# Inverse roots by Ln and Exp on ScalarE, and the first pairs' value products in four pieces

## The chip, the cores and the metric

The kernel runs on one core of a Trainium2 chip. Its time is device microseconds of one execution. Before the change it is 1099.2 us, the median of three runs (1098.22 to 1101.14); lower is better.

## The reference

```python
def _attn_ref(q, k, v, g_q, g_k):          # q, k, v: 8 x 12 x 448 x 64, float32
    def rmsnorm(x, g):
        rms = np.sqrt(np.mean(x * x, axis=-1, keepdims=True) + 1e-06)
        return x / rms * g
    q_n, k_n = (rmsnorm(q, g_q), rmsnorm(k, g_k))
    scores = 1.0 / np.sqrt(64) * np.matmul(q_n, k_n.transpose(0, 1, 3, 2))
    scores = scores - np.max(scores, axis=-1, keepdims=True)
    attn = np.exp(scores)
    attn = attn / (np.sum(attn, axis=-1, keepdims=True) + 1e-09)
    return np.matmul(attn, v)
def _moe_ref(x, w1, w2, w3, w_out):        # x: 3584 x 768 from the heads, weights 768 x 768, float64
    h = np.maximum(np.maximum(x @ w1, x @ w2), x @ w3)
    return h @ w_out
```

The weights come as 64-bit floats; the kernel turns their bits into 32-bit floats itself.

## The kernel before, in words

Two heads of one batch make a **pair** `g`; there are 48, six to a batch. The 448 queries of a pair are worked in four chunks `c` of 112. Each pair is written out as twelve **beats** (`beat(g, i)`, i from 0 to 11), three to a chunk, and `k = 4 * g + c` counts the chunks. The order of every engine's instructions is the order in which the beats issue them; an engine works its queue strictly in this order. `later(n, work)` issues work at the end of the beat that comes n beats on.

For each chunk, TensorE makes the scores of both heads (L545 or L553) into one of two buffers, VectorE takes the row maxima (L562), ScalarE scales them (L570) and makes two exponentials with their sums (L579). The scores of a chunk are issued one chunk ahead.

The first six pairs (`PLAIN = 6`, the **plain** pairs) work in float32: rows of keys and queries are transposed by TensorE (`turn_whole`, L463) and copied by ScalarE (`keep_whole`, L475 and L477), the exponentials are transposed by TensorE (L602) and copied (L611), and the value products (`add_values`, L692) are made in one block of eight matmuls in beat 4 of the next pair. Their result in `av` is multiplied by the inverse sums, which take this way: `guard_sums` (L619, ScalarE, beat 1), `inverse_sums` (L623, VectorE, beat 2), `spread_sums` (L631, TensorE, beat 5), `keep_sums` (L641, ScalarE, beat 6, the tile `by`), `scale_plain` (L711, VectorE, beat 8). `finish` (L717 ScalarE, L718 VectorE one beat later) splits the result into two float16 halves `xt`. From pair 6 on the work is in float16 halves: `upper_weights` (L648 and L652 on VectorE, L655 on ScalarE), `lower_weights` (L665 on VectorE), transposes by DMA; the values are scaled by GpSimd (L517) in beat 9 and cast by ScalarE (L525) in beat 11.

The norms of pair g + 2 are made while pair g runs: `squares` (L365, GpSimd) in beats 0 and 3, `sum_squares` (L372, VectorE) in beats 2 and 5, `inv_rms` in beats 5 and 7. The last is two GpSimd instructions each for keys and for queries, a scaling (L383) and a power with the exponent -0.5 (L387). `scale_k` (L419, L423) and `scale_q` (L394) follow in beats 8 and 9 on GpSimd. Pairs 0 and 1 are made ahead of the first beat, pair 0 with its squares on ScalarE and its scaling on VectorE.

Beside that runs the decoding of the weights, a block every four beats up to pair 5 and every eight then: SP loads `raw` (two buffers), ScalarE rescales it (L188), VectorE decodes it in three steps (L196, L200, L205), and for the input weights ScalarE (L268, L269) and GpSimd (L272) split it into halves. The feed-forward matmuls (L732, L796) are put into the beats by a fixed table of thirds once a batch's six pairs are done, from pair 6 on.

## Time and profile before

| | |
|---|---|
| median of three runs | 1099.2 us |
| profiled execution, its own time | 1099.43 us |
| span of the profiled execution | 1097.6 us |
| TensorE busy | 1011.4 us (92%) |
| VectorE busy | 755.7 us (69%) |
| ScalarE busy | 771.8 us (70%) |
| GpSimd busy | 704.2 us (64%) |
| powers on GpSimd (L387, 96 of them) | 154.2 us |

The shares are averages over parts with different limits, so they are read by stretches of the span. In rows of groups stand the count of instructions, their busy time and the mean of one in ns. In rows of a timeline stand start and length in us, and in brackets the idle time ahead with what ended it. Rows of waits give who waited for whom, the total in us, the number of times and the longest.

### The profile page before, as it was taken

The numbers are of one execution on the slowest core, as the hardware profiler recorded it, in microseconds if no ns is written. First come the engines' busy times: TensorE is split into PE (matmuls) and PEld (weight loads), VectorE is DVE, ScalarE is ACT, GpSimd is POOL, SyncE is SP. The second block draws the span as 40 slices with busy tenths as digits, with TensorE's granted clock in tenths as the row PEclk, the third lists the DMA queues.
The fourth block names the chain that finished last, engine by engine and source line by source line (L and its number), as shares of the span: only waits on it lengthen the run. The fifth ranks groups of instructions, "written<-read, shape, count | busy, mean of one in ns | idle before, by whom it ended". The sixth has DMA issues, their size and how long they took to land. (4 is left out here: it accounts for less than half of the span.)

```text
span 1097.6 us, 18387 instructions
## 1 busy us (share of the span) xinstructions
PE 1011.4 (92%) x6168; PEld 499.4 (45%) x6168; DVE 755.7 (69%) x1390; ACT 771.8 (70%) x1767; POOL 704.2 (64%) x805
## 2 busy tenths in 40 slices
PE   4678769888899999999999999999999999999998
PEld 2333334334444454444544454444444554445554
DVE  4799988888767676777677767777676766761110
ACT  4598888767878687787877787777777787863101
POOL 5477988866767777677777776777777677610000
PEclk9697869999999999999999999999999999999999
DMA  5554566855887779778887798787877797553002
GB/s 152 164 168 149 131 183 135 192 116 121 164 156 143 145 153 179 152 148 144 168 156 147 138 168 172 148 145 155 174 145 140 140 178 142 108 100 73 1 1 57
DMA packets 426493, 152.28 MB, mean 139 GB/s; under 512 B 372896, under 2 KB 422048, under 8 KB 426400
## 3 DMA queue, kind: packets, MB, share of 16 engines
q1 hardware_dynamic: 425888, 150.95, 67.7%
q8 instruction: 48, 0.79, 0.3%
q14 instruction: 45, 0.37, 0.1%
q10 hardware_dynamic: 512, 0.18, 0.1%
HBM read 51.97 MB, written 11.01 MB: 57 GB/s over the span
## 5 line engine op out<-in xcount | busy, mean ns | idle before, releaser
L732 PE MATMUL acc<-xt,w_sb 128*128 128x448 f16 x2592 | 516.8, 355 | 0.0
L732 PEld LDWEIGHTS <-w_sb 128*128 128x128 f16 x2592 | 244.1, 98 | 259.3 <-issue 47.9
L579 ACT ACTIVATE sc<-sc,nm,down 112x448 f32<-112x448 f32 x336 | 234.2, 697 | 11.2
L562 DVE TENSOR_REDUCE sc<-sc 112x2 f32<-112x896 f32 x192 | 209.6, 1092 | 46.0 <-PE sc L553 44.7
L655 ACT ACTIVATE pp<-sc,rs 112x448 f16<-112x448 f32 x336 | 194.8, 632 | 46.6 <-ACT sc L579 40.9
L665 DVE SCALAR_TENSOR_TENSOR pp<-sc,rs,pp 112x448 f16<-112x448 f32 x336 | 212.9, 675 | 3.4 <-ACT pp L655 2.9
L387 POOL TENSOR_TENSOR ri<-ri,half_neg 128x7 f32<-128x7 f32 x96 | 154.2, 1606 | 8.0
L553 PE MATMUL sc<-kt,qt 64*112 64x448 f16 x1008 | 131.9, 367 | 28.8 <-DVE pp L665 25.0
L570 ACT ACTIVATE nm<-sc,down 112x2 f32<-112x2 f32 x192 | 50.7, 264 | 147.5 <-DVE sc L562 146.1
L796 PE MATMUL acc<-wo_sb,ht 128*128 128x384 f16 x864 | 151.0, 329 | 1.5 <-DVE ht L756 0.8
L761 POOL COPY hx<-ht 128x128 f16<-128x128 f16 x48 | 15.5, 323 | 197.1 <-DVE ht L756 191.1
L796 PEld LDWEIGHTS <-ht 128*128 128x128 f16 x864 | 81.6, 99 | 67.2 <-issue 13.5
L703 PE MATMUL av<-pt,vp 128*64 128x448 f16 x1008 | 108.3, 356 | 0.0
L553 PEld LDWEIGHTS <-qt 64*112 64x112 f16 x1008 | 54.8, 126 | 98.3 <-issue 57.8
L648 DVE TENSOR_SCALAR rs<-sc 112x2 f32<-112x2 f32 x168 | 26.6, 158 | 94.6 <-ACT sc L579 94.6
L440 POOL TENSOR_TENSOR kp<-kn,kp 128x512 f16<-128x512 f32 x42 | 50.0, 1191 | 58.9 <-ACT kp L434 58.9
L703 PEld LDWEIGHTS <-vp 128*64 128x64 f16 x1008 | 49.6, 108 | 55.7 <-issue 30.0
L718 DVE SCALAR_TENSOR_TENSOR xt<-av,xt 128x448 f16<-128x448 f32 x42 | 26.2, 625 | 70.8 <-ACT xt L717 70.8
L372 DVE TENSOR_REDUCE ss<-sq 128x7 f32<-128x448 f32 x96 | 60.9, 635 | 10.6 <-ACT sq L363 6.6
L531 POOL TENSOR_TENSOR vp<-vr,vp 128x448 f16<-128x448 f32 x42 | 43.8, 1044 | 30.3 <-ACT vp L525 30.2
L440 POOL TENSOR_TENSOR qp<-qn,qp 112x512 f16<-112x512 f32 x42 | 49.2, 1173 | 19.8 <-ACT qp L434 19.8
L517 POOL TENSOR_SCALAR vr<-vr,v_up 128x448 f32<-128x448 f32 x42 | 61.1, 1456 | 0.0
(112 smaller groups left out, 1200.4 us busy)
## 6 DMA issues: line engine op xcount, KB each, us to landing
raw<-in_moe_w_dram SPq DMA_DIRECT2D x18, 768.0 KB, 4.5
qr<-in_q_dram SPq DMA_DIRECT2D x48, 224.0 KB, 3.1
vr<-in_v_dram SPq DMA_DIRECT2D x96, 96.0 KB, 2.6
kr<-in_k_dram SPq DMA_DIRECT2D x95, 96.0 KB, 3.1
raw<-in_moe_w_out_dram SPq DMA_DIRECT2D x6, 768.0 KB, 5.0
pt<-pp SPq DMA_TRANSPOSE x168, 4.0
out_dram<-osb SPq DMA_DIRECT2D x8, 336.0 KB, 3.2
out_dram<-osb SPq DMA_DIRECT2D x8, 288.0 KB, 3.6
```

The source lines that it names most:

```text
L372: nc.vector.tensor_reduce(sums[g % 2][:sq.shape[0], KQ[what]], sq, axis=AX, op=ALU.add)
L387: nc.gpsimd.tensor_tensor(out=ri, in0=ri, in1=half_neg[:, at], op=ALU.pow)
L440: nc.gpsimd.tensor_tensor(out=parts[:, 1], in0=n, in1=parts[:, 0], op=ALU.subtract)
L517: nc.gpsimd.tensor_scalar(out=vr, in0=vr, scalar1=v_up[:, g // NP:g // NP + 1], scalar2=None, op0=ALU.mult,)
L553: nc.tensor.matmul(sc[:QP, h, :S], qt[rows, qp, c], kt[rows, kp, KEYS[h]], start=n == 0, stop=n == len(TERMS) - 1,)
L562: nc.vector.tensor_reduce(sc[:QP, 0, S + 8:S + 10], sc[:QP, :, :S], axis=AX, op=ALU.max, negate=True)
L579: nc.scalar.activation(to, sc[:QP, h, :S], AF.Exp, bias=nm[:, h:h + 1], scale=down[:QP], accum_out=total,)
L655: nc.scalar.activation(pp[:, 0, h], sc[:QP, h, :S], AF.Copy, scale=rs[:, h:h + 1])
L665: nc.vector.scalar_tensor_tensor(out=pp[:, 1, h], in0=sc[:QP, h, :S], scalar=rs[:, h:h + 1], in1=pp[:, 0, h], op0=ALU.mult, op1=ALU.subtract,)
L703: nc.tensor.matmul(av[half, :S], vp[rows, group, vpart], pt[rows, 7 * wp + group], start=u == 0 and n == 0, stop=u == 3 and n == len(TERMS ...
L732: nc.tensor.matmul(acc[:, :S], wt[:, wp, c], xs[c][:, xp], start=(c == 0 and n == 0), stop=(c == NCT - 1 and n == 2),)
L796: nc.tensor.matmul(acc[:, :HW], lhs, wo_sb[:, f, wp, half * HW:(half + 1) * HW], start=(f == 0 and n == 0), stop=(f == NFT - 1 and n == 2),)
```

## The change

The change does five things.

- **Powers.** `inv_rms` goes. `mean_squares` (beat 4) scales and shifts all 15 sums of a pair in one instruction, `power` (beat 6) takes Ln and then Exp with a scale of -0.5 on ScalarE, `newton` (beat 8) corrects the result by one Newton step: four small instructions on GpSimd, three on VectorE for pairs 0 and 1. The squares move to beats 0 and 1 and their sums to beats 2 and 3. The table of functions that holds Ln and Exp is chosen at the start.
- **Scale of the plain scores.** The constant part of the scale goes into the gain that the transposed queries are multiplied with, so that plain exponentials take scale 1.0 and their row maxima go straight into `nm`; L570 and the scale tile `down` serve only pairs from 6 on. `prep_gain` moves to beat 4 of pair 0.
- **Value products.** For pairs 0 to 4 the eight matmuls are issued two at a time in beats 4, 7, 8 and 10; `scale_plain` goes to beat 11, and `finish` to the first beat after that.
- **Inverse sums.** The guard goes to beat 10 and the inverse to beat 11 of the pair itself; the spreading matmuls to beat 2 and the copy to beat 4 of the next pair.
- **Start.** Pair 1's powers and scaling are issued in beats 0 and 1; pair 1's transposes come in beats 4 and 7 of pair 0 instead of 1 and 4.

```diff
+    nc.scalar.preload_act_table_set("natural_log_exp_and_others")
     nc.scalar.activation(warm, warm, AF.Exp)
...
-    def inv_rms(g, what):
...
-        nc.gpsimd.tensor_scalar(
-            out=ri, in0=sums[g % 2][:, at], scalar1=1.0 / D / QK_UP ** 2,
-            scalar2=RMS_EPS / QK_UP ** 2, op0=ALU.mult, op1=ALU.add,
-        )
-        nc.gpsimd.tensor_tensor(out=ri, in0=ri, in1=half_neg[:, at], op=ALU.pow)
+    def mean_squares(g):
+        s = st[g]
+        s["ms"] = sb.tile([P, 15], F32, name="ms", bufs=2)
+        (nc.gpsimd if g > 1 else nc.vector).tensor_scalar(
+            out=s["ms"], in0=sums[g % 2], scalar1=1.0 / D / QK_UP ** 2,
+            scalar2=RMS_EPS / QK_UP ** 2, op0=ALU.mult, op1=ALU.add,
+        )
+    def power(g):
+        s = st[g]
+        ri = sb.tile([P, 15], F32, name="ri", bufs=2)
+        nc.scalar.activation(ri, s["ms"], AF.Ln)
+        nc.scalar.activation(ri, ri, AF.Exp, scale=-0.5)
...
+    def newton(g):
...
+        if g > 1:
+            nc.gpsimd.tensor_tensor(out=t, in0=ms, in1=ri, op=ALU.mult)
+            nc.gpsimd.tensor_tensor(out=t, in0=t, in1=ri, op=ALU.mult)
+            nc.gpsimd.tensor_scalar(
+                out=t, in0=t, scalar1=-0.5, scalar2=1.5, op0=ALU.mult, op1=ALU.add
+            )
+            nc.gpsimd.tensor_tensor(out=ri, in0=ri, in1=t, op=ALU.mult)
+            return
...
     def row_max(g, c):
+        if g < PLAIN:
+            to = s["nm", c] = sb.tile([QP, 2], F32, name="nm", bufs=3)
+        nc.vector.tensor_reduce(to, sc[:QP, :, :S], axis=AX, op=ALU.max, negate=True)
     def softmax(g, c):
...
+            nm, by = s.pop(("nm", c)), 1.0
+        else:
+            nm, by = sb.tile([QP, 2], F32, name="nm", bufs=3), down[:QP]
+            nc.scalar.activation(nm, sc[:QP, 0, S + 8:S + 10], AF.Copy, scale=by)
...
+    power(0)
+    newton(0)
     scale_k(0)
...
+    nc.scalar.activation(
+        gain_c, column[:, 0:1], AF.Copy, scale=1.0 / QK_UP ** 2 / float(D) ** 0.5
+    )
...
+    later(0, lambda: power(1))
+    later(1, lambda: newton(1))
+    later(1, lambda: scale_k(1))
+    later(1, lambda: scale_q(1))
+    later(4, prep_gain)
...
+        if g < PLAIN:
+            if i == 10:
+                guard_sums(g)
+            if i == 11:
+                inverse_sums(g)
         if 0 <= w < PLAIN:
             if i == 2:
-                inverse_sums(w)
-            if i == 5:
                 spread_sums(w)
-            if i == 6:
+            if i == 4:
                 keep_sums(w)
-            if i == (8 if w < PLAIN else 9):
+            if i == (8 if w == PLAIN - 1 else 11):
                 scale_plain(w)
+        if 0 <= w < PLAIN - 1 and i in (4, 7, 8, 10):
+            add_values(w, [(4, 7, 8, 10).index(i)])
+        elif w >= PLAIN - 1 and i == (4 if w < PLAIN else 7):
             add_values(w)
...
+        if 0 <= w < PLAIN - 1 and i == 11:
+            later(1, lambda: finish(w, x_of[w // NP]))
...
+            if i in (0, 1):
+                squares(n, "kq"[i])
+            if i in (2, 3):
+                sum_squares(n, "kq"[i - 2])
+            if i == 4:
+                mean_squares(n)
+            if i == 6:
+                power(n)
             if i == 8:
+                newton(n)
                 scale_k(n)
```

The change moves lines of the file: L562 becomes L590, L570 L602, L579 L607, L623 L651, L665 L693, L711 L740, L718 L747, L196 L195, L200 L199, L205 L204, L372 L371. Three places show what the queues become. The rows are in the order in which an engine works them; `x2` is two alike.

VectorE at the start, from pair 1's sums of squares (`ss_87` before, `ss_86` now) to pair 2's, before:

```order
L372 TENSOR_REDUCE ss_87<-sq 128x7
L372 TENSOR_REDUCE ss_87<-sq 112x8
L562 TENSOR_REDUCE sc<-sc 112x2 x2
L372 TENSOR_REDUCE ss_86<-sq 128x7
L170 TENSOR_REDUCE v_rows<-vr 128x1
```

and now:

```order
L371 TENSOR_REDUCE ss_86<-sq 128x7
L371 TENSOR_REDUCE ss_86<-sq 112x8
L378 TENSOR_SCALAR ms<-ss_86 128x15
L590 TENSOR_REDUCE nm<-sc 112x2
L404 SCALAR_TENSOR_TENSOR newton<-ms,ri 128x15
L407 TENSOR_TENSOR newton<-newton,ri 128x15
L408 SCALAR_TENSOR_TENSOR ri<-newton,ri 128x15
L590 TENSOR_REDUCE nm<-sc 112x2
L371 TENSOR_REDUCE ss_85<-sq 128x7
```

Newton's three steps for pair 1 stand between the first two row maxima.

VectorE in a plain pair, where pair 1's products are finished. Before, in pair 2 from beat 8 on (`sc<-sc` is the row maximum):

```order
L562 TENSOR_REDUCE sc<-sc 112x2
L711 TENSOR_TENSOR av<-av,by 128x448
L200 SCALAR_TENSOR_TENSOR w_sb<-raw,w_sb 128x768
L170 TENSOR_REDUCE v_rows<-vr 128x1
L205 SCALAR_TENSOR_TENSOR w_sb<-raw,w_sb 128x768
L718 SCALAR_TENSOR_TENSOR xt<-av,v_up,xt 128x448
```

and now, from beat 11 of pair 2 on (`nm<-sc` is the row maximum):

```order
L590 TENSOR_REDUCE nm<-sc 112x2
L651 RECIPROCAL sum<-sum 112x8
L740 TENSOR_TENSOR av<-av,by 128x448
L195 TENSOR_SCALAR w_sb<-raw 128x768
L258 TENSOR_SCALAR w_most<-most 128x1
L261 RECIPROCAL w_up<-w_most 128x1
L262 TENSOR_SCALAR w_up<-w_up 128x1
L199 SCALAR_TENSOR_TENSOR w_sb<-raw,w_sb 128x768
L747 SCALAR_TENSOR_TENSOR xt<-av,v_up,xt 128x448
L204 SCALAR_TENSOR_TENSOR w_sb<-raw,w_sb 128x768
```

The second half of `xt` moved one beat on and behind other decoding steps, and the reciprocal of the pair's sums now stands right behind a row maximum.

VectorE in a pair from 6 on, around the sums of squares of the queries (`ss_87`, now `ss_86`), before:

```order
L562 TENSOR_REDUCE sc<-sc 112x2
L665 SCALAR_TENSOR_TENSOR pp<-sc,rs,pp 112x448 x2
L648 TENSOR_SCALAR rs<-sc 112x2
L652 RECIPROCAL rs<-rs 112x2
L372 TENSOR_REDUCE ss_87<-sq 112x8
L746 TENSOR_TENSOR acc<-acc,m 128x448
```

and now:

```order
L590 TENSOR_REDUCE sc<-sc 112x2
L693 SCALAR_TENSOR_TENSOR pp<-sc,rs,pp 112x448 x2
L371 TENSOR_REDUCE ss_86<-sq 112x8
L676 TENSOR_SCALAR rs<-sc 112x2
L680 RECIPROCAL rs<-rs 112x2
L775 TENSOR_TENSOR acc<-acc,m 128x448
```

The sum moved from behind the two steps of the weights' sums to ahead of them. SP's loads and DMA transposes keep their order, and there is one table load in the changed program as in the one before.

More of the change, by code (lines that the diff above doesn't have):

```diff
@@ L869, in prep_gain @@
     def prep_gain():
-        nc.vector.tensor_tensor(out=gain, in0=gains[:, 0], in1=gains[:, 1], op=ALU.mult)
         row_largest(g_top[:, 0:1], gain)
@@ L899, in qknorm_attention_maxout_ffn_kernel @@
         )
[L900 to L902 removed]
+    turn_whole(0, "q")
+    nc.scalar.activation(
+        gain_c, column[:, 0:1], AF.Copy, scale=1.0 / QK_UP ** 2 / float(D) ** 0.5
+    )
     for what in "kq":
```

72 lines of the change are left out of this document (29 added, 43 removed).

## The prediction

> **What bounds the kernel now.** I read the page first, then the busy times by stretches, one stretch per pair (cut where the copy of `by`, L641, starts), then the waits of VectorE, then the timelines.
>
> ```profile
> span 1097.6 us, 18387 instructions
> PE 1011.4 (92%) x6168; PEld 499.4 (45%) x6168; DVE 755.7 (69%) x1390; ACT 771.8 (70%) x1767; POOL 704.2 (64%) x805
> ```
>
> ```profile
> 40.40:54.07 13.67, 12.22 (x71) 6.72 (x71) 12.20 (x17) 10.90 (x28) 4.49 (x5) 0.77 0.55 168
> 54.07:71.33 17.26, 13.16 (x86) 6.51 (x86) 16.81 (x24) 16.25 (x40) 11.86 (x12) 1.00 0.55 167
> 71.33:93.30 21.97, 17.66 (x91) 9.01 (x91) 20.60 (x26) 19.35 (x45) 18.73 (x15) 0.77 0.45 142
> 93.30:114.04 20.74, 16.42 (x88) 8.34 (x88) 20.19 (x25) 19.34 (x44) 17.66 (x15) 0.84 0.46 145
> 114.04:136.40 22.36, 15.88 (x80) 7.57 (x80) 20.92 (x25) 19.43 (x45) 20.12 (x18) 0.77 0.61 158
> 136.40:161.72 25.32, 14.60 (x76) 8.35 (x76) 22.20 (x35) 20.13 (x45) 24.13 (x21) 0.68 0.63 164
> ...
> 500.00:700.00 200.00, 197.70 (x1259) 96.93 (x1256) 141.66 (x280) 152.44 (x358) 141.96 (x171) 1.00 0.84 157
> ```
>
> After the stretch come its length and the busy time of PE, PEld, DVE, ACT, POOL. From 500 to 700 us PE works 197.7 of 200: there the matmuls are the bound, and nothing that VectorE, ScalarE or GpSimd gain is worth anything. PE's other idle time lies ahead of that. From 40.40 to 161.72 us the six rows give DVE 112.9 of 121.3 busy: in the plain pairs VectorE is the bound, and only its idle 8.4 us can be won by letting the others run better. Whatever is won there moves the whole PE-bound rest forward, since its order on PE stays as it is.
>
> ```profile
> DVE xt L718 <- ACT xt L717: 4.0, 3, 1.5
> DVE w_sb L196 <- ACT raw L188: 2.0, 1, 2.0
> ...
> DVE av L711 <- ACT by L641: 0.7, 2, 0.3
> ```
>
> These are VectorE's waits in the same 121 us (total, times, longest). The first and the last belong to lines that the change moves.
>
> **The start: nothing.** Pair 0's powers leave GpSimd. The timeline (start, length, engine, line, what ended the idle time):
>
> ```profile
> 0.72 1.28 ACT L133 ACT_TABLE_LOAD   x1 [0.72 <-PEq L1046]
> ...
> 5.80 0.69 DVE L372 TENSOR_REDUCE ss<-sq 112x8 f32<-112x512 f32 x1 [0.46 <-ACT sq L363]
> 9.01 0.35 DVE L419 TENSOR_TENSOR kn<-kr,ri 128x192 f32<-128x192 f32 x1
> 14.66 1.10 DVE L562 TENSOR_REDUCE sc<-sc 112x2 f32<-112x896 f32 x1 [0.23 <-PE sc L545]
> 17.56 0.51 POOL L419 TENSOR_TENSOR kn<-kr,ri 128x192 f32<-128x192 f32 x1
> 18.85 0.29 POOL L423 TENSOR_TENSOR kn<-kr,ri 64x64 f32<-64x64 f32 x1
> 19.17 0.81 SPq L342 DMA_DIRECT2D kr<-in_k_dram  x2
> 35.31 3.42 SPq L223 DMA_DIRECT2D raw<-in_moe_w_dram  x2
> 40.41 0.88 ACT L188 ACTIVATE raw<-raw 128x768 f32<-128x768 f32 x1 [3.60 <-DMA raw<-in_moe_w_dram]
> ```
>
> The last sums are done at 6.49. Mean squares, Ln, Exp and three VectorE steps, six small dependent instructions of some 0.2 us each (priced below), end near 7.9, where `kn` now starts at 9.01: 1.1 us sooner. But pair 1's powers now stand on ScalarE behind the first two exponentials. The first row maximum moves by 0.9 (the column of gains now stands among the transposes) from 14.66 to 13.8 and ends at 14.9; two exponentials (1.4), Ln and Exp (0.5), Newton's three steps (0.6) end at 17.4, where GpSimd's `kn` starts at 17.56 today. The load of `kr` at 19.17 starts as soon as that `kn` has ended (18.85 + 0.29), and behind it SP issues loads without a gap up to the raw weights at 35.31, for which ScalarE stands still until 40.41. So the gain of 1.1 us is given back at 17.5, and at 40.4 I expect 0, with bounds of -1.0 and +0.8. The next row maximum is queued behind Newton's steps on VectorE, and behind that exp(0,1), which has 2 us in hand since its key rows no longer stand ahead of it.
>
> **The plain pairs: -3.8 us.**
>
> The groups of the page (count, busy, mean ns of one) and, for the plain exponentials, those from 20 to 180 us:
>
> ```profile
> L570 ACT ACTIVATE nm<-sc,down 112x2 f32<-112x2 f32 x192 | 50.7, 264 | 147.5 <-DVE sc L562 146.1
> ...
> L579 ACT ACTIVATE e<-sc,nm,down 112x448 f32<-112x448 f32 x46 | 32.9, 719 | 0.8
> ```
>
> Two rows of the view of L717 (shortest, median, longest ns), and two of GpSimd's groups:
>
> ```profile
> L717 ACT ACTIVATE xt<-av x42: 535/543/545, 192.8 to 1005.7; 128x448 f16<-128x448 f32 x42
> L717 ACT ACTIVATE xt<-av,v_up x6: 627/630/634, 57.0 to 166.7; 128x448 f16<-128x448 f32 x6
> ...
> L383 POOL TENSOR_SCALAR ri<-ss 128x8 f32<-128x8 f32 x48 | 13.3, 277 | 13.1 <-DVE ss L372 13.1
> L387 POOL TENSOR_TENSOR ri<-ri,half_neg 128x7 f32<-128x7 f32 x96 | 154.2, 1606 | 8.0
> ```
>
> ScalarE, per plain pair: four `nm` go, 4 x 0.264 = 1.06. Eight exponentials lose their scale taken from a tile; L717 with and without such a scale differs by 0.087, so 8 x 0.087 = 0.70. Ln and Exp of 128x15 come in. No row shows them: between 0.1 and 0.3 each, and I take 0.25, near the 0.264 of the smallest L570. The sum is -1.26 us of about 19.4. ScalarE has no wait on the table of functions beyond the first: the order of the changed program holds one table load.
>
> GpSimd, per pair: two scalings and two powers, 2 x 0.277 + 2 x 1.606 = 3.8, become five small instructions, 5 x 0.28 = 1.4. That is -2.4 us, but VectorE waits for GpSimd nowhere in the list above, so it is worth 0 here.
>
> The value products are the same matmuls in four places, so PE's sum stays. Today they stand as one block ahead of the transposes of the query rows, for which ScalarE waits (L477). That is worth time only where VectorE then waits for ScalarE.
>
> VectorE, per pair: nothing is removed or added from pair 2 on; L623, L711 and L718 change places. The wait of 4.0 us in L718 came from a place where only L205 stood between the maximum and it. Now, behind the maximum of beat 11, there stand the reciprocal, L711, L196, three small ones and L200, and ScalarE needs only two exponentials and L717 (2 x 0.63 + 0.63 = 1.9 us) in that time, on a queue 1.26 us shorter. VectorE's groups from 40.4 to 161.7 us, and the view of L205:
>
> ```profile
> L200 DVE SCALAR_TENSOR_TENSOR w_sb<-raw,w_sb 128x768 uint32<-128x768 uint32 x16 | 17.8, 1113 | 0.2
> ...
> L205 DVE SCALAR_TENSOR_TENSOR w_sb<-raw,w_sb 128x768 uint32<-128x768 uint32 x16 | 26.1, 1634 | 0.2
> ...
> L711 DVE TENSOR_TENSOR av<-av,by 128x448 f32<-128x448 f32 x5 | 3.1, 619 | 0.7 <-ACT by L641 0.7
> ...
> L205 DVE SCALAR_TENSOR_TENSOR w_sb<-raw,w_sb x18: 936/954/4291, 28.5 to 147.1; 128x768 uint32<-128x768 uint32 x18
> ```
>
> L711 and L200 alone are 1.7 us. So the 4.0 goes, and the 0.7 of L711 too, as `by` is made seven beats ahead instead of two. Against it stands one new wait: the reciprocal now needs the exponentials of beat 9 and the guard of beat 10, one maximum behind them; 0.2 us a pair in five pairs, 0.9 us. -4.7 + 0.9 = -3.8. The bounds: -6.4 (all 8.4 but the raw weights' 2.0) and +3. The upper one is from these rows: L205 at its undisturbed 0.95 would take 15.2 us in 16 and took 26.1, L200 takes 17.8 against the same 15.2. The 13.5 us over it are VectorE held up while GpSimd streams; the same GpSimd streams come at other moments now, and a fifth more or less is 3 us.
>
> ```profile
> 87.51 1.48 POOL L387 TENSOR_TENSOR ri<-ri,half_neg 128x7 f32<-128x7 f32 x1
> 87.72 0.54 DVE L196 TENSOR_SCALAR w_sb<-raw 128x768 uint32<-128x768 uint32 x1
> ...
> 88.29 0.96 DVE L200 SCALAR_TENSOR_TENSOR w_sb<-raw,w_sb 128x768 uint32<-128x768 uint32 x1
> ```
>
> The powers themselves don't hold VectorE up: both decode steps run at full speed inside the 1.48 us of one. So taking them away frees nothing. The Trainium skill ("SBUF — State Buffer", the section on its two physically separate sides) says otherwise: GpSimd and VectorE share a port pair as an exclusive lock, held for the whole instruction. By that rule the powers would hold it too; this trace doesn't agree for so small an operand.
>
> **Pairs 6 to 11: -1 us.**
>
> ```profile
> DVE rs L648 <- ACT sc L579: 11.0, 15, 1.4
> ...
> PE sc L553 <- DVE pp L665: 13.7, 9, 3.2
> ```
>
> From 162 to 306 us PE still waits 13.7 us for VectorE's second halves of the weights. Per pair one sum of squares moves from behind the reciprocal of L652 to ahead of L648, where VectorE waits 0.7 us for the exponentials anyway. It takes 0.68 as the row at 5.80 (0.69). At most 6 x 0.68 = 4 us come out; only one of four maxima in a pair has it ahead, so I take a quarter, 1 us, bounds -4 and +1. Ln and Exp stand between the exponentials and L655, which waits for VectorE's reciprocal there.
>
> **The rest: 0.** ScalarE gets 0.5 us a pair, GpSimd loses 2.4, under a PE that is 98.9% busy. The bounds are -0.5 and +2; the loss above that is the fourth case below. The loads on SP keep their order.
>
> The sum: 0 - 3.8 - 1 + 0 = -4.8. The profiled execution took 1099.43 (span 1097.6 and 1.8 around it), 0.2 over the median of 1099.2. Predicted: 1094.6.
>
> **The rivals.** One: VectorE stays just as full, because what its waits give up it loses to GpSimd's streams, which now crowd on it as GpSimd is no longer held back by the powers. For it: 13.5 us are lost there today, three times what I count on. Against it: the streams' order hardly changes. The time: -4.8 + 3 to 4 = 1098, 1096 to 1101.
>
> Two: more than the listed waits goes. All 6.4 us in the plain pairs, 3 in pairs 6 to 11, and 1 at the start: 1089. For it: ScalarE, PE and VectorE wait for each other in turn, so a lighter ScalarE may let every wait go. The rule on the port lands here as well, as a mechanism of this kernel: were the powers 3.2 of some 19 busy us of GpSimd that hold VectorE up, a sixth of the 13.5 us, 2.3 us, would go too, 1092; the rows above speak against it, 3 in 100.
>
> Three, the slower one: the second halves of the powers now hang on ScalarE's order.
>
> ```profile
> 612.00 0.51 POOL L419 TENSOR_TENSOR kn<-kr,ri 128x192 f32<-128x192 f32 x1
> 613.03 0.13 ACT L579 ACTIVATION_READ_ACCUMULATOR sc<-sc,nm,down 112x1 f32 x1
> 616.03 1.41 POOL L517 TENSOR_SCALAR vr<-vr,v_up 128x448 f32<-128x448 f32 x1
> 620.11 0.58 ACT L525 CAST vp<-vr 128x448 f16<-128x448 f32 x1
> ```
>
> Ln follows the third chunk's exponentials (613.2 in this pair), Newton on GpSimd takes 4 x 0.28 behind it, so `kn` starts at 614.8 instead of 612.0, and `vr` ends at 620.2 instead of 617.4, just behind the moment (620.1) at which ScalarE wants it in L525. Queued behind L525 are the next pair's exponentials. It decides from the point where that is later than L525 by more than PE's slack, 2.3 us in 200 or 0.23 a pair. At 0.25 us a pair in 42 pairs it costs 10.5: 1105. Against it: ScalarE is 76% busy there, and L525 slips by its own 0.5 us too.
>
> Four: Ln isn't what the program computes with cheaply, each use loading a table (1.28 us for the load at 0.72, 96 of them, 123 us, 1218); the single load in the order leaves it 1 in 100.
>
> **How the numbers follow.** Forecast 46 in 100 (1091.5 to 1098), rival one 22, two 19, three 12, four 1. A measurement of this kernel tells about 0.3%, 3.3 us, from no change: below 1095.9 is faster, above 1102.5 slower. Faster: two thirds of the forecast (31), a tenth of rival one (2), all of two (19), 52. Slower: three and four and 2 of rival one, 15. Same: 33. The range 1087.5 to 1101 holds the forecast, nearly all of rival one and more than half of two.
>
> **What would show it.** In the profile after: the raw weights' wait of ScalarE still ends near 40.4 (start right); L718's wait on L717 gone from VectorE's list, and the stretch between the copies of `by` equal to VectorE's busy time (plain pairs right); L205's mean still near 1.6 us (rival one if 1.9, rival two if 1.3); PE's waits on L665 from 162 to 306 at 12 to 13 us; L525 without a wait for `vr` (else rival three). The prediction is wrong if the plain pairs are bound by something other than VectorE, or if the collisions change by more than a fifth.

## The result, and the profile after

The change makes the kernel slower. After: 1106.31 us, the median of five runs (1104.79 to 1108.47), against 1099.67 of the kernel before on the same chip (1098.22 to 1102.68): a ratio of 1.0058, 95% interval 1.0037 to 1.0079, or 6.6 us. Predicted were 1094.6, and a range that ended at 1101. The profiled execution of the changed kernel took 1108.47 with a span of 1106.7; it is the slowest of its five, 2.2 us above their median (that of undo_p, further down, is 3.3 above its own), so the parts read from traces don't add up to the differences of the medians. All lines of "after" are from it.

The page's line of busy times:

```profile
PE 1014.1 (92%) x6168; PEld 498.5 (45%) x6168; DVE 763.1 (69%) x1397; ACT 777.2 (70%) x1839; POOL 583.8 (53%) x843
```

GpSimd lost 120 us of work, TensorE does the same 6168 matmuls, and the span grew by 9.1. To find where, I cut both traces at the starts of the same row maxima: pair 1's first, pair 6's first (the border after the plain pairs), pair 8's first. Before, then after (start and end, length, busy time of PE, PEld, DVE, ACT, POOL, then the granted clock and DMA):

```profile
38.19:142.32 104.13, 78.79 (x432) 39.97 (x430) 96.23 (x120) 91.06 (x203) 78.62 (x66) 0.81 0.53 157
142.32:193.91 51.59, 42.08 (x226) 20.48 (x227) 45.88 (x79) 42.81 (x89) 45.48 (x41) 0.83 0.71 157
```

```profile
39.58:143.35 103.77, 76.94 (x428) 38.94 (x426) 94.88 (x118) 83.97 (x190) 62.52 (x66) 0.84 0.51 154
143.35:202.54 59.19, 41.83 (x227) 18.91 (x227) 51.19 (x81) 45.05 (x96) 40.99 (x48) 0.86 0.59 138
```

Three numbers stand in the cuts. At pair 1 the changed kernel is 1.4 us late (39.58 against 38.19). The plain pairs take the same time, 103.77 against 104.13, and even that only because pair 4's last two VectorE instructions (0.6 and 0.7 us) now lie behind the border. Pairs 6 and 7 take 59.19 instead of 51.59, 7.6 us more. The lag at pair 8 is 8.6 us, and 9.0 at pair 47 (972.90 before, 981.92 after), so the 779 us between them add 0.4.

TensorE's bound there is what it was, 197.66 of 200 us:

```profile
508.70:708.70 200.00, 197.66 (x1260) 96.89 (x1256) 142.19 (x280) 155.53 (x378) 118.66 (x182) 1.00 0.77 156
```

**The start.** The timeline of VectorE, and the two rows that answer to those shown of before, the load of `kr` and ScalarE's work on the raw weights:

```profile
16.62 0.65 DVE L404 SCALAR_TENSOR_TENSOR newton<-ms,ri 128x15 f32<-128x15 f32 x1 [1.76 <-ACT ri L388]
17.30 0.96 DVE L407 TENSOR_TENSOR newton<-newton,ri 128x15 f32<-128x15 f32 x1
18.29 0.17 DVE L408 SCALAR_TENSOR_TENSOR ri<-newton,ri 128x15 f32<-128x15 f32 x1
...
20.15 0.33 SPq L341 DMA_DIRECT2D kr<-in_k_dram  x1
...
40.66 0.88 ACT L187 ACTIVATE raw<-raw 128x768 f32<-128x768 f32 x1 [3.69 <-DMA raw<-in_moe_w_dram]
```

Newton's first two steps for pair 1 took 0.65 and 0.96 instead of 0.17, beside GpSimd's squares of pair 2, and the load of `kr` starts 1.0 us later than before (20.15 against 19.17). ScalarE comes to the raw weights, the mark that the prediction named, only 0.25 us later (40.66 against 40.41).

**The plain pairs.** VectorE's waits in them (total, times, longest), the list that began with L718's 4.0 us before:

```profile
DVE sum L651 <- ACT sum L647: 7.3, 5, 1.8
DVE xt L747 <- ACT xt L746: 1.1, 1, 1.1
```

The wait of `xt` has gone from 4.0 to 1.1 and that of `by` is gone, as predicted; the reciprocal waits 7.3 us for the guard (L647), where 0.9 was predicted. The first of its five waits:

```profile
42.19 0.22 ACT L647 ACTIVATE sum<-sum 112x8 f32<-112x8 f32 x1
...
42.44 0.20 DVE L651 RECIPROCAL sum<-sum 112x8 f32<-112x8 f32 x1 [1.78 <-ACT sum L647]
```

Ahead of this guard ScalarE had stood still for the raw weights until 40.66, so these 1.8 us are in the place of the 2.0 that L196 waited for them before. All of VectorE's listed waits in the plain pairs come to 8.4 us, against 7.2 before.

ScalarE's instructions came out close to their prices: a plain exponential takes 0.633 instead of 0.719, Ln and Exp 0.21 each (0.25 was taken), and there is no further table load. ScalarE's groups from 20 to 180 us (count, busy, mean ns of one, idle time ahead):

```profile
L607 ACT ACTIVATE e<-sc,nm 112x448 f32<-112x448 f32 x46 | 28.8, 633 | 23.6 <-DVE nm L590 23.5
...
L388 ACT ACTIVATE ri<-ri 128x15 f32<-128x15 f32 x7 | 1.5, 214 | 0.2
```

**Pairs 6 and 7.** VectorE is busy 51.19 instead of 45.88 us and idle 8.0 instead of 5.7. Part of the busy time is pair 4's end (1.3). The rest is decoding. The same cuts with the steps on the raw weights alone, before and after:

```profile
142.32:193.91 51.59, 14.32 (x12) 0.83 0.71 157
```

```profile
143.35:202.54 59.19, 18.29 (x13) 0.86 0.59 138
```

That is 4.0 us more, of which one step more in the cut is 0.95. 4.0 + 1.3 + 2.3 is the 7.6. The longest of these steps, with what GpSimd did meanwhile:

```profile
176.18 1.03 POOL L555 TENSOR_TENSOR vp<-vr,vp 128x448 f16<-128x448 f32 x1
177.17 1.64 POOL L271 TENSOR_TENSOR w_sb<-w_sb 128x768 f16<-128x768 f32 x1
178.77 1.03 POOL L364 TENSOR_TENSOR sq<-qr 112x512 f32<-112x512 f32 x1
179.77 1.86 POOL L463 TENSOR_TENSOR kp<-kn,kp 128x512 f16<-128x512 f32 x1
...
176.60 4.02 DVE L199 SCALAR_TENSOR_TENSOR wo_sb<-raw,wo_sb 128x768 uint32<-128x768 uint32 x1
```

These GpSimd instructions follow each other without a gap, and a step of 0.95 us takes 4.02. It begins within the first of them and ends at 180.62, 0.85 us into the fourth, which is longer by 0.7 (1.86 against the 1.16 that the same instruction took at 154.32). So each engine stands still for the other here; why VectorE gets its turn at the fourth and not sooner, the rows don't show. Before, that step took 1.51 us (at 171.81).

The trace therefore leaves two suspects: the reciprocal's wait (7.3 us, most of it new) and what the powers' move did to GpSimd's order. They are told apart by undoing parts.

### The profile page after: what moved, and what is told of

It reads as the page before. It is cut to its first block, busy times and chain, and to the rows that moved or that the text cites. A ratio compares the mean times of both kernels' runs of the same rounds, so it can differ in the third digit from the quotient of the medians.

```text
span 1106.7 us, 18538 instructions
## 1 busy us (share of the span) xinstructions
PE 1014.1 (92%) x6168; PEld 498.5 (45%) x6168; DVE 763.1 (69%) x1397; ACT 777.2 (70%) x1839; POOL 583.8 (53%) x843
## 5 line engine op out<-in xcount | busy, mean ns | idle before, releaser
L607 ACT ACTIVATE sc<-sc,nm,down 112x448 f32<-112x448 f32 x336 | 234.4, 698 | 11.2
L590 DVE TENSOR_REDUCE sc<-sc 112x2 f32<-112x896 f32 x168 | 183.5, 1092 | 59.4 <-PE sc L577 59.1
L693 DVE SCALAR_TENSOR_TENSOR pp<-sc,rs,pp 112x448 f16<-112x448 f32 x336 | 213.0, 676 | 3.5 <-ACT pp L683 2.7
L602 ACT ACTIVATE nm<-sc,down 112x2 f32<-112x2 f32 x168 | 44.3, 264 | 125.2 <-DVE sc L590 123.6
L397 POOL TENSOR_TENSOR newton<-ms,ri 128x15 f32<-128x15 f32 x46 | 12.4, 269 | 137.4 <-ACT ri L388 137.4
L747 DVE SCALAR_TENSOR_TENSOR xt<-av,xt 128x448 f16<-128x448 f32 x42 | 26.2, 625 | 71.5 <-ACT xt L746 71.5
L371 DVE TENSOR_REDUCE ss<-sq 128x7 f32<-128x448 f32 x96 | 61.2, 640 | 6.8 <-ACT sq L362 6.8
L429 POOL TENSOR_TENSOR qn<-qn,gain 112x512 f32<-112x512 f32 x42 | 55.3, 1317 | 3.3
```

Of the source, the lines that this page charges most:

```text
L371: nc.vector.tensor_reduce(sums[g % 2][:sq.shape[0], KQ[what]], sq, axis=AX, op=ALU.add)
L429: nc.gpsimd.tensor_tensor(out=n, in0=n, in1=gain[:QP].rearrange("p (o d) -> p o d", o=1).broadcast_to([QP, 8, D]), op=ALU.mult,)
L590: nc.vector.tensor_reduce(to, sc[:QP, :, :S], axis=AX, op=ALU.max, negate=True)
L607: nc.scalar.activation(to, sc[:QP, h, :S], AF.Exp, bias=nm[:, h:h + 1], scale=by, accum_out=total,)
L693: nc.vector.scalar_tensor_tensor(out=pp[:, 1, h], in0=sc[:QP, h, :S], scalar=rs[:, h:h + 1], in1=pp[:, 0, h], op0=ALU.mult, op1=ALU.subtract,)
```

## The experiments

Every kernel was timed beside the kernel before on its own chip, whose median lay between 1099.05 and 1100.34. The ratios, with their 95% intervals:

| run | what it is | median, us | ratio to before |
|---|---|---|---|
| after | the change | 1106.31 | 1.0058 (1.0037 to 1.0079) |
| undo_i | change, inverse sums at the old beats | 1105.55 | 1.0049 (1.0036 to 1.0062) |
| undo_v | change, value products in one block | 1105.43 | 1.0053 (1.0040 to 1.0066) |
| undo_p | change, powers on GpSimd | 1096.45 | 0.9971 (0.9962 to 0.9980) |
| early | change, Ln and Exp a beat sooner | 1104.04 | 1.0035 (1.0021 to 1.0049) |
| nopow | before without its powers | 1093.09 | 0.9939 (0.9922 to 0.9956) |
| spacer | change plus idle powers | 1109.44 | 1.0086 (1.0071 to 1.0101) |
| from2 | change, pairs 0 and 1 with powers | 1104.57 | 1.0041 (1.0026 to 1.0056) |
| late_i | undo_p, reciprocal two beats later | 1092.59 | 0.9932 (0.9917 to 0.9947) |
| sq_early | undo_p, squares at the change's beats | 1093.42 | 0.9954 (0.9939 to 0.9969) |
| lean | change without scaling and Newton | 1096.74 | 0.9982 (0.9970 to 0.9994) |
| newton_late | change, Newton two beats later | 1101.74 | 1.0028 (1.0004 to 1.0052) |
| lean_late | lean, from2 and late_i together | 1090.30 | 0.9927 (0.9912 to 0.9942) |
| no_newton | change without Newton's step | 1098.41 | 0.9981 (0.9967 to 0.9996) |
| ms_late | change, Ln from the sums, Newton kept | 1107.35 | 1.0064 (1.0042 to 1.0086) |
| best_pow | undo_p, sq_early and late_i together | 1089.38 | 0.9904 (0.9872 to 0.9936) |
| newton_dve | change, Newton on VectorE | 1105.23 | 1.0052 (1.0037 to 1.0067) |
| four_idle | lean plus four idle steps | 1098.90 | 0.9992 (0.9982 to 1.0003) |

Differences below are differences of ratios, times 1099.7.

### Which part of the change costs?

**undo_i.**

```diff
-        if g < PLAIN:
-            if i == 10:
-                guard_sums(g)
-            if i == 11:
-                inverse_sums(g)
         if 0 <= w < PLAIN:
+            if i == 1:
+                guard_sums(w)
             if i == 2:
+                inverse_sums(w)
+            if i == 5:
                 spread_sums(w)
-            if i == 4:
+            if i == 6:
                 keep_sums(w)
```

> The changed kernel with the inverse sums back at their old beats (guard 1, inverse 2, spreading 5, copy 6 of the next pair), the rest as changed. Theory A: the loss is the new wait of the reciprocal on the guard, 8.6 us in six plain pairs. Then the row maximum at the border to pair 6 comes some 6 to 8 us sooner than 143.4 and the time is 1098 to 1100. Theory B: the loss arises in pairs 6 and 7 (143 to 203 us), because GpSimd idles for Ln and Exp and then works in one burst against VectorE's decoding. Then the lag there stays and the time is 1104 to 1106.

Measured: 1105.55, 1.0 us off the change, intervals overlapping. The reciprocal's wait is gone, and other waits stand in its place in the plain pairs:

```profile
DVE xt L747 <- ACT xt L746: 4.2, 2, 2.4
DVE av L740 <- PE av L721: 1.6, 4, 0.7
DVE w_sb L195 <- ACT raw L187: 1.0, 1, 1.0
DVE sc L590 <- ACT e L607: 0.7, 1, 0.7
```

That is 7.5 us of waits in all, where the change has 8.4. Theory A falls: with the old beats back, other waits stand where this one stood.

**undo_v.** The calls `add_values(w)` in beat 4, `scale_plain` in beat 8 and `finish` in beat 9 stand again for all plain pairs.

> The changed kernel with the value products of pairs 0 to 4 again in one block at beat 4, their scaling at beat 8 and finish at beat 9. Theories A and B: neither the reciprocal's wait (8.6 us) nor GpSimd's burst hangs on it, 1105 to 1107; the waits of xt on ScalarE come back by up to 2 us, or go since the copies of the inverse sums come sooner. Theory C: the finish of pair 4, pushed past the border to pair 6 (1.3 us of VectorE, more of ScalarE), is what fills pair 6; then 1101 to 1103.

Measured: 1105.43, no difference. Theory C falls: pair 4's end behind the border isn't the cause.

**undo_p.** `mean_squares`, `power` and `newton` go, `inv_rms` and its beats are back, for pairs 0 and 1 too:

```diff
-            if i in (0, 1):
-                squares(n, "kq"[i])
...
-            if i == 6:
-                power(n)
+            if i in (0, 3):
+                squares(n, "kq"[i // 3])
+            if i in (2, 5):
+                sum_squares(n, "kq"[i // 3])
+            if i in (5, 7):
+                inv_rms(n, "kq"[i // 7])
             if i == 8:
-                newton(n)
                 scale_k(n)
```

> The changed kernel with the powers back on GpSimd at their old beats, pair 0 and 1 too, the other parts as changed. Theory B: GpSimd no longer idles and bursts in pairs 6 and 7, the lag of 7.6 us from 143 to 203 goes and most of the 1.4 us at the start: 1097 to 1099. Theory A: the wait on the guard stays, ScalarE has no Ln and Exp ahead of it, 1104 to 1107.

Measured: 1096.45, below even the kernel before. The powers' move costs 9.6 us, the other parts together win 3.2. Theory B is right about the part. It is not right about the place. The same cuts of undo_p:

```profile
36.66:137.00 100.34, 75.69 (x430) 38.25 (x428) 92.51 (x118) 82.42 (x181) 70.76 (x63) 0.86 0.53 161
137.00:193.54 56.54, 42.02 (x222) 18.91 (x221) 50.15 (x81) 44.02 (x90) 46.84 (x45) 0.82 0.66 146
```

Against the kernel before, pair 1's first maximum comes 1.5 us sooner and the plain pairs take 3.8 us less, but pairs 6 and 7 still take 5.0 us more, with 17.43 us of decoding against 14.32 and pair 4's end behind the border. Against these cuts the change loses 2.9 us at the start, 3.4 in the plain pairs and 2.7 in pairs 6 and 7. The next runs ask what in the powers' move does it.

**early.** `power(n)` at beat 5 instead of 6.

> The changed kernel with Ln and Exp from pair 2 on one beat sooner (beat 5 instead of 6), Newton where it was. Theory B: GpSimd's wait of 5.2 us for Exp in pair 6 shrinks by about a beat (2 to 3 us) and with it the burst behind it; 1102 to 1104. Theory A: no difference, 1105 to 1107.

Measured: 1104.04, 2.5 us, intervals overlapping in part. In this trace GpSimd waits 2.3 us for Exp from 20 to 205 us instead of 23.0, and still most of the loss is there.

### What about the powers' move costs?

**nopow.**

```diff
-            out=ri, in0=sums[g % 2][:, at], scalar1=1.0 / D / QK_UP ** 2,
-            scalar2=RMS_EPS / QK_UP ** 2, op0=ALU.mult, op1=ALU.add,
+            out=ri, in0=sums[g % 2][:, at], scalar1=0.0,
+            scalar2=QK_UP, op0=ALU.mult, op1=ALU.add,
         )
-        nc.gpsimd.tensor_tensor(out=ri, in0=ri, in1=half_neg[:, at], op=ALU.pow)
```

> The kernel before with its 96 powers on GpSimd left out and nothing in their place (the scaling ahead of them writes a constant, so the norms count as 1; the rest runs on those values). Theory D: a power is GpSimd time that leaves VectorE's decoding alone, a gap between streams that hold it up; without the powers the streams crowd on VectorE, and the kernel with less work is not faster: 1099 to 1104. Theory E: what costs is only that GpSimd waits for Exp on ScalarE; with neither power nor wait the kernel is faster: 1093 to 1098.

Measured: 1093.09, 6.7 us faster than before. **spacer** is the opposite, pure extra work in the changed kernel:

```diff
+            if i in (5, 7):
+                at = KQ["kq"[i // 7]]
+                nc.gpsimd.tensor_tensor(out=idle_out[:, at], in0=idle_in[:, at],
+                                        in1=half_neg[:, at], op=ALU.pow)
```

> The changed kernel with the old powers on GpSimd added at their old beats, from a constant into a tile that nobody reads (pure extra work, 1.6 us each). Theory D: the gaps between the streams are back, a good part of the 9.9 us that the powers' move cost is won: 1099 to 1103. Theory E: GpSimd comes out of its wait for Exp with more work: 1106 to 1110.

Measured: 1109.44, 3.1 us slower than the change. Theory D falls in both runs: the powers were no useful gap. Both runs lie in theory E's ranges, and leaving out all the powers is worth 6.7 us, where the prediction had it at nothing. (In nopow's trace 2.5 us of it are won ahead of pair 1.) Theory E's own reason, the wait for Exp, is still to be tested.

**from2.** `inv_rms` for pairs 0 and 1 ahead of the first beat, as before; the rest as changed.

> The changed kernel with the powers of pairs 0 and 1 made on GpSimd as before, those from pair 2 on by Ln, Exp and Newton. At the first row maximum of pair 1 the changed kernel is 2.9 us behind the one with all powers on GpSimd; if the start's loss is carried to the end, this one takes 1103 to 1104, if it is absorbed behind it (VectorE's collisions change with it), 1105 to 1107.

Measured: 1104.57. The start's share is 1.9 us, with overlapping intervals; some 7.7 of the 9.6 belong to the pairs from 2 on.

**sq_early** (undo_p with `squares` in beats 0 and 1 and `sum_squares` in 2 and 3) asks whether the squares' new beats are it.

> The kernel with the powers back on GpSimd, its squares and their sums now at the changed kernel's beats (0 and 1, 2 and 3). Theory F: of the 9.9 us that the powers' move costs, these beats are a part, since VectorE works on the sums sooner and GpSimd's squares come in one piece: 1099 to 1104. If the beats don't matter: 1095 to 1098, as without them.

Measured: 1093.42, better than undo_p by 1.9 us with overlapping intervals, below both ranges. Theory F falls; the new beats do no harm. So the loss is to be sought between the sums and the keys.

**lean.**

```diff
-        nc.scalar.activation(ri, s["ms"], AF.Ln)
+            nc.scalar.activation(
+                ri, sums[g % 2], AF.Ln, bias=eps, scale=1.0 / D / QK_UP ** 2
+            )
...
-            if i == 4:
-                mean_squares(n)
...
             if i == 8:
-                newton(n)
                 scale_k(n)
```

> The changed kernel where from pair 2 on Ln takes the sums themselves (its scale and a bias tile do the scaling and the shift), and the Newton step is left out; GpSimd then has neither the scaling that waits for VectorE's sums nor Newton's four steps, and its multiplication of the keys waits for Exp alone. Theory E (the stops in GpSimd's queue): one of two stops goes, 1099 to 1103. If ScalarE's share (Ln and Exp in its order, and the wait for them) is the cost: 1104 to 1107.

Measured: 1096.74, 8.4 us better than the change, more than theory E allowed, although GpSimd waits 61.0 us for Exp from 20 to 205 us here, against 23.0 in the change. So theory E's reason, that wait, is not the cost. Ln and Exp with the wait for them stand in the powers' place at 1.2 us more than undo_p (overlapping intervals); they don't win the 6.7 us of nopow either. What costs is the scaling on GpSimd or Newton's four steps. Two runs take them one at a time. **no_newton** keeps the scaling and drops `newton(n)`; **ms_late** drops the early scaling, and issues `mean_squares(n)` right ahead of `newton(n)` in beat 8.

> The changed kernel with Newton's step left out from pair 2 on, the scaling on GpSimd (the stop for VectorE's sums) kept. Theory G: Newton's four steps ahead of the keys are the cost (3.4 us of GpSimd a plain pair in the trace, ahead of the next streams); then 1097 to 1099. Theory H: the stop at the scaling is the cost, 1104 to 1107.

> The changed kernel with Newton kept, but Ln taking the sums themselves; the scaling that Newton needs is issued right ahead of Newton, long after the sums are there. Theory G: 1104 to 1108 (five small steps ahead of the keys instead of four). Theory H: 1097 to 1099.

Measured: 1098.41 without Newton, 1107.35 with Newton and without the early scaling. Theory G holds, H falls: Newton's step costs 8.5 us, the scaling nothing that can be told (0.9981 against 0.9982).

**newton_late.** `newton` and `scale_k` in beat 10, `scale_q` in 11.

> The changed kernel with Newton and the scaling of keys and queries two beats later (beats 10 and 11), so that GpSimd comes to them after Exp has been made. Theory E: GpSimd's 18.7 us of waiting for Exp in the first 220 us go, its other streams are no longer held behind them: 1101 to 1104. If that wait is only idle time that costs nothing: 1105 to 1108, or more where the next pair's transposes then wait for keys.

Measured: 1101.74, 3.3 us better with overlapping intervals, in theory E's range. The place seems to matter, but two beats win less than half of what leaving the step out wins.

### What about Newton's step costs?

Newton's four groups on GpSimd in the changed kernel from 40 to 143 us (count, busy, mean ns):

```profile
L398 POOL TENSOR_TENSOR newton<-newton,ri 128x15 f32<-128x15 f32 x5 | 7.2, 1450 | 0.4
...
L402 POOL TENSOR_TENSOR ri<-ri,newton 128x15 f32<-128x15 f32 x5 | 4.2, 849 | 0.4
...
L397 POOL TENSOR_TENSOR newton<-ms,ri 128x15 f32<-128x15 f32 x5 | 2.5, 495 | 9.3 <-ACT ri L388 9.3
...
L399 POOL TENSOR_SCALAR newton<-newton 128x15 f32<-128x15 f32 x5 | 1.9, 375 | 0.4
```

That is 15.8 us in five pairs, with the gaps between the steps (1.2) 3.4 a pair, where a step takes 0.22 undisturbed. The timeline in pair 3 (ScalarE's and GpSimd's rows, then VectorE's):

```profile
95.29 0.21 ACT L388 ACTIVATE ri<-ri 128x15 f32<-128x15 f32 x1
95.65 0.22 POOL L397 TENSOR_TENSOR newton<-ms,ri 128x15 f32<-128x15 f32 x1 [1.36 <-ACT ri L388]
95.95 1.76 POOL L398 TENSOR_TENSOR newton<-newton,ri 128x15 f32<-128x15 f32 x1
97.79 0.22 POOL L399 TENSOR_SCALAR newton<-newton 128x15 f32<-128x15 f32 x1
98.09 1.01 POOL L402 TENSOR_TENSOR ri<-ri,newton 128x15 f32<-128x15 f32 x1
99.18 0.51 POOL L442 TENSOR_TENSOR kn<-kr,ri 128x192 f32<-128x192 f32 x1
...
100.47 0.29 POOL L446 TENSOR_TENSOR kn<-kr,ri 64x64 f32<-64x64 f32 x1
...
96.69 0.93 DVE L199 SCALAR_TENSOR_TENSOR w_sb<-raw,w_sb 128x768 uint32<-128x768 uint32 x1
98.08 0.94 DVE L204 SCALAR_TENSOR_TENSOR w_sb<-raw,w_sb 128x768 uint32<-128x768 uint32 x1
...
103.27 3.84 DVE L199 SCALAR_TENSOR_TENSOR w_sb<-raw,w_sb 128x768 uint32<-128x768 uint32 x1
```

L398 ends within 0.1 us of VectorE's L199, L402 within 0.1 us of L204: the small steps, too, stand until VectorE's decoding step is through. (L398 already stands for 0.7 us before L199 begins, beside a row maximum; what holds it there isn't shown.) From Exp's end (95.50) to the first of the four key steps (`kn`) 3.7 us pass, and to the end of the last one 5.3. The same place without Newton:

```profile
92.68 0.21 ACT L388 ACTIVATE ri<-ri 128x15 f32<-128x15 f32 x1
92.97 0.55 POOL L442 TENSOR_TENSOR kn<-kr,ri 128x192 f32<-128x192 f32 x1 [1.30 <-ACT ri L388]
93.49 1.69 POOL L446 TENSOR_TENSOR kn<-kr,ri 64x64 f32<-64x64 f32 x1
...
95.72 0.89 POOL L446 TENSOR_TENSOR kn<-kr,ri 64x64 f32<-64x64 f32 x1
...
100.24 2.83 DVE L199 SCALAR_TENSOR_TENSOR w_sb<-raw,w_sb 128x768 uint32<-128x768 uint32 x1
```

Here the first key step follows 0.1 us behind Exp, but now two key steps take 1.69 and 0.89 us instead of 0.29, beside the same two decoding steps, and the last is through 3.7 us behind Exp. So Newton delays the keys by 1.6 us in this pair. Behind the keys GpSimd runs its streams in one piece (weights, queries, squares), and the next pair's decoding step meets them in both kernels, for 1.9 us over its 0.95 without Newton and 2.9 with it. The cuts of no_newton, whole and then with the decoding alone:

```profile
39.64:138.88 99.24, 71.55 (x428) 35.63 (x428) 92.37 (x119) 84.02 (x190) 58.95 (x50) 0.92 0.52 160
138.88:194.30 55.42, 42.39 (x231) 19.66 (x230) 49.35 (x81) 44.94 (x96) 37.77 (x36) 0.85 0.64 147
```

```profile
39.64:138.88 99.24, 46.63 (x46) 0.92 0.52 160
138.88:194.30 55.42, 16.70 (x13) 0.85 0.64 147
```

In the plain pairs 4.5 us go (103.77 to 99.24): 2.5 are decoding (49.08 us of 46 steps to 46.63), 2.0 are VectorE's waits. In pairs 6 and 7 3.8 go: 1.6 decoding, 1.9 waits. The granted clock in the plain pairs is 0.92 here and 0.84 in the change, but that isn't the cause: in lean's trace it is 0.83, and they take 99.70 us. Is it the time that the small steps hold GpSimd, or that the keys hang on them? **four_idle** puts four small multiplications ahead of the keys of lean, into a tile that nobody reads:

```diff
             if i == 8:
+                for step in range(4):
+                    nc.gpsimd.tensor_tensor(
+                        out=idle_out[:, step], in0=idle_in, in1=idle_in, op=ALU.mult
+                    )
                 scale_k(n)
```

> The kernel where Ln takes the sums and Newton is left out (1096.7), with four small multiplications of a constant 128x15 tile on GpSimd ahead of the keys, into a tile that nobody reads. If the cost is the time that such steps hold GpSimd's queue, VectorE's streams holding them up too: 1102 to 1107. If it is the chain of dependence behind Exp: the four run while GpSimd waits for Exp anyway, and nothing changes: 1095.5 to 1098.

Measured: 1098.90 against lean's 1096.74, intervals overlapping: at most a small part of it. They run while GpSimd waits for Exp (in pair 3 the four take 0.73 us, and 5.8 us of waiting follow). So what costs is a step *between Exp and the keys*, not the time of four small steps on GpSimd. **newton_dve** makes the step on VectorE:

> The changed kernel with Newton's step on VectorE for all pairs (three steps of 0.17 us that the trace shows for pairs 0 and 1), Ln, Exp and the scaling where they are. If the cost is GpSimd's time for the four steps: 1097 to 1101, VectorE's own 0.5 us a plain pair included. If it is the longer chain from Exp to the keys, or VectorE now waits for Exp at that place: 1103 to 1108.

Measured: 1105.23, no better than on GpSimd that can be told. The step there takes 0.5 us, but stands behind a row maximum, and the collisions grew. Its cuts, decoding alone:

```profile
39.68:142.68 103.00, 51.55 (x46) 0.86 0.50 155
142.68:201.56 58.88, 19.96 (x13) 0.83 0.63 139
```

51.55 + 19.96 = 71.5 us against 67.4 in the change (49.08 + 18.29) and 63.3 without Newton; in exchange VectorE is idle for 9.0 us instead of 16.9 in the change and 12.9 without Newton. So a step between Exp and the keys costs about 8 us on either engine. Shown is that it does; on GpSimd the time comes out as longer decoding steps and waits of VectorE in about equal parts, on VectorE as longer decoding alone. Not settled is why collisions fall as they do for each order. The delay of the keys alone doesn't say it: in pair 3 newton_dve's keys are through 4.7 us behind Exp, 1.0 later than without the step, and newton_late's 7.3 us behind it, although newton_late is not the slower one.

### Can the two good parts be added?

**late_i.** The reciprocal's wait was hidden in undo_i by others; with the powers on GpSimd it is tried again, another way:

```diff
             if i == 10:
                 guard_sums(g)
-            if i == 11:
-                inverse_sums(g)
         if 0 <= w < PLAIN:
+            if i == 1:
+                inverse_sums(w)
```

> The kernel of the run with the powers back on GpSimd, with the reciprocal issued two beats later (beat 1 of the next pair, the guard stays at beat 10), behind the next work of VectorE instead of ahead of it. If the 8.5 us of the reciprocal's waits can be won: 1090 to 1093. If VectorE's collisions or pairs 6 and 7 take it again: 1095 to 1097, no different from that run.

Measured: 1092.59, 4.3 us better than undo_p. VectorE's waits in the plain pairs:

```profile
DVE xt L724 <- ACT xt L723: 3.0, 3, 1.3
DVE w_sb L196 <- ACT raw L188: 1.7, 1, 1.7
```

Of the 7.3 us that VectorE waits for the guard in the plain pairs of undo_p, as in the change, none is left. So the wait was worth about half of what it showed. What this edit wins with Newton's step still there was not run.

**lean_late** joins lean, from2 and late_i, **best_pow** undo_p, sq_early and late_i.

> The changed kernel with Ln from the sums and no Newton step from pair 2 on, the powers of pairs 0 and 1 on GpSimd, and the reciprocal at beat 1 of the next pair: the best form of the change with logarithms that the runs so far suggest. If Ln and Exp on ScalarE can be as good as the power on GpSimd, once neither stops GpSimd's queue: 1089 to 1093. If not: 1095 to 1100.

> The kernel with the powers on GpSimd, the squares and sums at the changed kernel's beats and the reciprocal at beat 1 of the next pair. The two steps won 3.0 and 3.9 us apart from each other over 1096.4. If they add up: 1089 to 1090.5. If both win the same time: 1092 to 1094.

Measured: 1090.30 and 1089.38. From the ratios best_pow should win 1.9 + 4.3 over undo_p, and wins 7.4 (the interval of best_pow alone is 3.5 us to each side): the two gains add up within that. Both kernels beat the one before, by 0.7% (0.6 to 0.9) and 1.0% (0.6 to 1.3); the two can't be told from each other, so Ln and Exp at their best here gain nothing over the powers. The cuts of best_pow:

```profile
37.34:132.57 95.23, 72.93 (x430) 36.69 (x428) 90.07 (x118) 81.93 (x180) 76.41 (x63) 0.89 0.56 169
132.57:185.10 52.53, 40.53 (x231) 19.32 (x230) 46.17 (x82) 44.35 (x92) 46.17 (x44) 0.87 0.69 158
```

The plain pairs take 95.2 us instead of 104.1, with the decoding at 44.45 instead of 48.90 us, and pairs 6 and 7 give only 0.9 back.

## Why the prediction was wrong

**What bounds the kernel: right.** VectorE was busy 94.88 of 103.77 us in the plain pairs, TensorE 197.66 of 200 from 508.7 on, and from pair 8's first row maximum to pair 47's every trace takes 776 to 780 us (779.0 before), so what is won or lost ahead of pair 8 mostly stays.

**The start: 0 predicted, 1.4 us lost** at pair 1's first row maximum; about 1.9 by from2. At the prediction's own mark, the raw weights, it looks right (0.25 us late, within the bound of +0.8), so that mark doesn't show the loss. The step that failed is "Newton's three steps (0.6)": two of them met GpSimd's squares and the three took 1.8 us, and `kn` starts at 18.55 instead of the 17.4 worked out. The chain behind it (SP's load, the raw weights) moved as described.

**The plain pairs: -3.8 predicted, -0.4 in the trace.** The removed waits came out (4.0 to 1.1 and 0.7 to 0), ScalarE's relief too. Two terms failed:

- *"One new wait ... 0.2 us a pair"* measured 1.5 a pair (7.3 in five, of which 1.8 are the raw weights' old wait under another name). The guard stands on ScalarE behind both exponentials of the last chunk, the turned exponentials and a rescaling of raw weights, and I counted only what VectorE has ahead, not what ScalarE has ahead of the guard. With the powers back on GpSimd, moving the reciprocal behind VectorE's next work wins 4.3 us (late_i).
- *"-2.4 us, but VectorE waits for GpSimd nowhere in the list above, so it is worth 0 here."* This is the step that turned the sign. The list of waits shows only semaphores; VectorE's dependence on GpSimd is also in the length of its decoding steps, and I had the row for it (13.5 us of such lengthening). The same step priced "five small instructions, 5 x 0.28 = 1.4" by their undisturbed time. Newton's four steps alone take 3.4 us a pair in the changed trace from 40 to 143 us, and they lie between Exp and the keys, on which GpSimd's order hangs: Newton's step costs 8.5 us (after against no_newton). For the powers alone, replaced by Ln and Exp without Newton, 0 was about right: lean is 1.2 us over undo_p, and the 6.7 us of nopow, which puts nothing in their place, don't come.

**The collisions**: the prediction allowed "a fifth more or less is 3 us" and took none. In the plain pairs that held for the change itself: 48.90 us of decoding before, 49.08 after. It is pairs 6 and 7 where they grew, 14.32 to 18.29 us, and there the prediction had looked only at sums of squares and TensorE's waits: **-1 predicted** for pairs 6 to 11, **+7.6 measured** in pairs 6 and 7. Of these 7.6 us 5.0 stand in undo_p's trace too, so most of this miss doesn't hang on the powers' move; beyond the decoding and pair 4's end its cause stays open. Without the powers' move undo_p is 3.2 us faster than before, near the 4.8 predicted for all, but in part by luck: its plain pairs win the 3.8 predicted, its start 1.5 that were not, and pairs 6 and 7 lose what should have been won.

**The rest: 0 predicted, +0.4 measured.** Right, though ScalarE's L549 (L525 before) now waits for `vr` 12 times, 14.3 us in all, against 3.0 us before.

**Rival three**, the slower one, named the right instructions (Ln behind the exponentials, Newton's four steps ahead of `kn`) and put their price at the wrong place: its waits came, under TensorE's bound they cost nothing, and what Newton cost lay in the pairs bound by VectorE. Its 1105 agrees with the result by chance. Rival one (collisions take back what waits give up, 3 to 4 us) has the size of the longer decoding in pairs 6 and 7 (4.0 us), but it spoke of the plain pairs, where the decoding stayed; rival two's size (1089) is reached by best_pow, another kernel, and some waits stay there. Rival four fell: one table load.

**The rule on the ports** weighed there was set aside after one look at the powers. Four decoding steps lie wholly inside a power in the trace of before, none more than 0.02 us over its shortest; in the lines of the prediction L200 only begins inside one and ends 0.26 us behind it, and it isn't longer either. The other way round a power is held: the one at 67.74 us begins 0.12 us behind an L200 and takes 2.18 us instead of 1.48. Other GpSimd instructions both hold and are held: L199's 4.02 us, and Newton's 0.22 us steps that take 1.76 and 1.01 until VectorE's step has ended. The Trainium skill ("SBUF — State Buffer", the section on its two physically separate sides) says that GpSimd and VectorE take a shared port pair as an exclusive lock for a whole instruction, and that the one that comes second fully blocks. The trace agrees with it in all of these cases but one: a power that is running doesn't hold up the decoding step that comes second. The rule should have been asked of the instructions that come in, not only of those that go.

## What to carry to other kernels

Price an added small instruction by how long its like takes beside the work that the other engine does at that moment, not by its shortest duration, and above all where a whole engine's order hangs on its result: four steps of 0.22 us cost 8.5 us here, four that nothing hung on cost at most a small part of that. An engine that no list of waits names can still hold the bound one up; look at the spread of the same instruction's durations before calling its relief worthless. And a wait taken away may only move (undo_i won 1.0 us, with overlapping intervals, of 7.3), so try it again in another way once the larger cause is out (4.3 us).

## What the runs showed of the hardware that I had not expected

- A 128x15 multiplication on GpSimd takes 0.22 us, and up to 1.76 us beside VectorE's decoding; a GpSimd power of 128x7 takes 1.48 and more and doesn't hold VectorE's decoding up, while a decoding step that was there first holds the power up. The row of before has shortest, median and longest in ns:

```profile
L387 POOL TENSOR_TENSOR ri<-ri,half_neg x96: 1478/1640/2178, 5.8 to 944.1; 128x7 f32<-128x7 f32 x48, 128x8 f32<-128x8 f32 x48
```

- Ln and Exp of 128x15 on ScalarE take 0.21 us each, so that the pair of them costs a quarter of one GpSimd power (1.6 us).
- Back-to-back GpSimd streams kept one VectorE step waiting through the rest of one instruction and two more (4.02 us instead of 0.95); the next was then held up by VectorE's step for 0.7 us.
